# A plus-one by a ones matmul in PSUM, the first chunk pairs scaled straight from its bank, and TensorE's work put in another order

## The chip, the cores and the metric

The kernel runs on one core of one Trainium2 chip. The metric is the device time in microseconds (us). TensorE does the matmuls and the transposes, VectorE and ScalarE the elementwise work. Each execution also has a mean granted clock of TensorE, between 0.5 and 1.0 of full speed at any moment.

## The reference

One block of a diffusion transformer in bf16: 2 samples of 256 tokens, width 1152 (9 chunks of 128), hidden width 4608, 2 heads. Only the first lines matter here:

```python
mod = (_silu(c) @ w_mod).reshape(B, 6, 1, D)
shift_a, scale_a, gate_a, shift_m, scale_m, gate_m = [mod[:, i] for i in range(6)]
h = _layernorm(x, axis=-1) * (1 + scale_a) + shift_a
qkv = (h @ wqkv).reshape(B, N, 3, H, Dh)
# ... attention, output projection, second LayerNorm, two large matmuls
```

The tokens lie in four tiles of 128 (tiles 0 and 1 belong to sample 0, tiles 2 and 3 to sample 1). Each tile is normalised, transposed chunk by chunk by TensorE, and multiplied by `1 + scale_a` on its way from PSUM to SBUF ("modulated"); then the key projection starts on those chunks while more of `w_mod` is still arriving.

## The kernel before

`scale_a` is worked out in four groups of chunks, as each group's weights land. A group is a row of tiny matmuls (2 columns each) into a PSUM tile, and one instruction that adds one while it copies the result to SBUF. The small PSUM tiles share two banks in turn.

```python
def aux_tile(shape, name, dt=FP32):
    return psum.tile(shape, dt, name=name, tag="aux", bufs=2)

KGROUPS = [(0, 2), (2, 4), (4, 6), (6, 9)]

def scale_group(g):
    k0, k1 = KGROUPS[g]
    pm = aux_tile([P, k1 - k0, B], "pm")
    for j in range(k0, k1):
        for k in range(KD):
            nc.tensor.matmul(
                pm[:, j - k0, :], w_scale_a[:, k, j * P:(j + 1) * P], sT[:, k, 0:B],
                start=(k == 0), stop=(k == KD - 1),
            )

    def add_one(eng):
        dst = scale_a[:, k0:k1, :]
        if eng == "d":
            nc.vector.tensor_scalar_add(dst, pm[:], 1.0)
        else:
            nc.scalar.activation(dst, pm[:], ACT.Identity, bias=one_t[:])

    return add_one

def modulate(pt, i, k, t0, j0, w, eng):      # hT0 chunk k = transposed tile * (1 + scale)
    ...

def k_step(k, c0=0, c1=T, m0=0, m1=KM1):     # key matmuls of chunk k, tokens c0..c1
    ...
```

The stretch that the change reorders (`"a"` is ScalarE, `"d"` is VectorE; `P` is 128, `N` is 256; `warm` issues matmuls on zeros that only keep TensorE busy):

```python
    pt_0 = transpose_x([0, 1], [0])
    warm(4, pwarm)
    ...
    norm1(1, 0, CUT, "d")
    stats_aggregate(2)
    norm1(0, CUT, D, "d")
    scale_group(0)("a")
    for k in range(2):
        modulate(pt_0, k, k, 0, 0, P, "a")
    warm(1, pwarm)
    pt_1 = aux_tile([P, 1, 8 * P], "pt", BF16)
    for k in range(2):
        transpose_into(pt_1, k, k, 1)
    for k in (2, 3):
        for t in range(TPB):
            transpose_into(pt_1, 2 * (k - 1) + t, k, t)
    for k in range(2):
        modulate(pt_1, 0, k, 1, k * P, P, "d")
    sqrt1(2)
    k_step(0, 0, P)
    k_step(1, 0, P)
    ...
    norm1(2, 0, CUT, "d")
    k_step(0, P, N)
    k_step(1, P, N)
    ...
    for k in range(2):
        transpose_into(pt_1, 6 + k, k, 2)
    for k in range(2):
        modulate(pt_1, 0, k, 2, (6 + k) * P, P, "a")
    scale_group(1)("a")
    sqrt1(3)
    for k in (2, 3):
        modulate(pt_1, 0, k, 0, 2 * (k - 1) * P, N, "d")
    k_step(0, N, N + P)
    k_step(1, N, N + P)
    recip1(3)
    norm1(3, 0, CUT, "d")
    k_step(2, 0, N)
    ...
```

## Time and profile before

| | before |
|---|---|
| median of the 3 runs on hand first | 243.79 us (243.61 to 243.87) |
| span of the profiled run | 242.1 us |
| TensorE busy | 235.3 us, 97% |
| first scale weights landed, second, third group | 9.09, 12.17, 15.26 us |
| third scale group starts on TensorE | 15.57 us |

The page lists an engine's busy time; at 97% TensorE, a change counts by what it does to TensorE's work and to its remaining idle time. The chain of waits, in order of time, lists start, duration, engine, tile and line; each row is what released the next. The lines of both views stand in the prediction.

### The profile page before, as it was taken

How to read it: one execution, taken by the hardware profiler on the slowest of the kernel's cores; microseconds unless marked ns; L12 is line 12 of the kernel's file. 1: busy time of each engine (PE TensorE's matmuls, PEld its weight loads, DVE VectorE, ACT ScalarE, POOL GpSimd, SP SyncE). 2: the span in 40 equal slices, each digit the busy share in tenths (PEclk: the TensorE clock that was granted, in tenths of full speed). 3: DMA queues.
4: the chain of work that ended last, by engine and by line, in shares of the span. 5: the costliest groups of instructions: out<-in, count | busy, mean ns of one | idle time of the engine just before them, and what ended most of it. 6: DMA issues, size and time to landing. Idle time of an engine off the chain costs nothing.

```text
span 242.1 us, 4031 instructions
## 1 busy us (share of the span) xinstructions
PE 235.3 (97%) x1698; PEld 142.7 (59%) x1698; DVE 93.4 (39%) x209; ACT 69.5 (29%) x138; POOL 32.0 (13%) x48
## 2 busy tenths in 40 slices
PE   8799999999999999999999999999999999999994
PEld 2486444466656666888844444444566656665573
DVE  2872550675694676720000019999002000000001
ACT  6532250543735174782222233322000000000000
POOL 1000400000310616300000000000314111111111
PEclk9999999999999999999999999999999999999999
DMA  6999999999999999799999999996891000000000
GB/s 223 324 330 360 379 344 247 326 372 284 254 322 361 380 255 208 208 219 327 327 328 249 191 274 328 327 326 188 245 286 39 19 16 16 20 20 27 19 19 16
DMA packets 76989, 54.48 MB, mean 225 GB/s; under 512 B 26011, under 2 KB 72491, under 8 KB 76971
## 3 DMA queue, kind: packets, MB, share of 16 engines
q1 hardware_dynamic: 76240, 53.02, 77.7%
q0 software_dynamic: 704, 1.20, 1.6%
q8 instruction: 13, 0.21, 0.4%
q14 instruction: 5, 0.04, 0.0%
q10 hardware_dynamic: 27, 0.00, 0.0%
HBM read 46.90 MB, written 1.19 MB: 199 GB/s over the span
## 4 chain that ended last, share of the span: by engine, by line
PE 91%; DMA 3%; ACT 2%; DVE 2%; issue 0%; SPq 0%; DVEq 0%
PE pacc L866 29%; PE pacc L802 29%; PE pacc L584 7%; PE pacc L705 6%; PE pacc L511 5%; PE pk L288 4%; DMA w_scale_a<-in_w_mod_dram 3%; PE pacc L519 2%; PE pk L318 2%; ACT hT L687 2%; PE pa L619 1%; PE ps_s L539 1%; PE pn L432 1%; PE pm L248 1%; PE pt L266 1%; PE pg L467 1%
## 5 line engine op out<-in xcount | busy, mean ns | idle before, releaser
L802 PE MATMUL pacc<-hT,w_f 128*128 128x256 bf16 (+1 forms) x432 | 70.5, 326 | 0.2 <-ACT hT L687 0.2
L866 PE MATMUL pacc<-w_f,gT 128*128 128x384 bf16 (+2 forms) x468 | 70.5, 314 | 0.0
L866 PEld LDWEIGHTS <-gT 128*128 128x128 bf16 x468 | 44.4, 98 | 26.2
L802 PEld LDWEIGHTS <-w_f 128*128 128x128 bf16 x432 | 42.2, 98 | 28.0 <-issue 0.4
L485 DVE SCALAR_TENSOR_TENSOR late<-w_gate_mT,late 128x1152 bf16<-128x1152 bf16 x18 | 24.4, 1358 | 36.8 <-DMA w_gate_mT<-in_w_mod_dram 36.2
L872 DVE TENSOR_TENSOR tmp<-pacc,gate 128x384 f32<-128x384 f32 (+2 forms) x13 | 6.8, 527 | 62.5 <-PE pacc L866 50.5
L840 ACT ACTIVATE gT<-pacc 128x512 bf16<-128x512 f32 x24 | 14.3, 597 | 32.3 <-PE pacc L802 32.3
L485 DVE SCALAR_TENSOR_TENSOR s_spill<-w_scale_m,s_b 128x1152 bf16<-128x1152 bf16 x12 | 16.3, 1357 | 8.5 <-DMA w_scale_m<-in_w_mod_dram 8.2
L705 PE MATMUL pacc<-w_o,big 128*128 128x384 bf16 (+2 forms) x117 | 17.9, 314 | 0.0
L874 POOL TENSOR_TENSOR o_sb<-tmp,x 128x384 bf16<-128x384 f32 (+1 forms) x12 | 11.7, 974 | 47.4 <-DVE tmp L872 47.4
L584 PE MATMUL pacc<-w_v,hT 128*128 128x384 bf16 x108 | 17.9, 326 | 0.0
L705 PEld LDWEIGHTS <-big 128*128 128x128 bf16 x117 | 11.0, 98 | 6.8 <-ACT big L627 0.2
L584 PEld LDWEIGHTS <-hT 128*128 128x128 bf16 x108 | 10.4, 98 | 7.0 <-issue 0.2
L288 PE MATMUL pk<-big,w_k 128*128 128x128 bf16 (+2 forms) x102 | 13.3, 278 | 0.0
L711 POOL TENSOR_TENSOR x<-tmp,x_sb 128x384 f32<-128x384 f32 (+1 forms) x11 | 9.8, 891 | 17.4 <-DVE tmp L710 9.5
L511 PE MATMUL pacc<-hT,w_q 128*128 128x512 bf16 x54 | 11.8, 379 | 0.1
L327 POOL DMA_DIRECT2D gates_dram<-grow x4 | 2.1, 521 | 70.8 <-DVE grow L826 70.8
L818 ACT ACTIVATE gT<-pacc 128x512 bf16<-128x512 f32 x12 | 6.9, 597 | 10.4 <-PE pacc L802 10.4
L288 PEld LDWEIGHTS <-w_k 128*128 128x128 bf16 x102 | 7.8, 98 | 3.0
L511 PEld LDWEIGHTS <-w_q 128*128 128x128 bf16 x54 | 5.3, 98 | 6.7 <-issue 0.4
L710 DVE TENSOR_TENSOR tmp<-pacc,gate 128x384 f32<-128x384 f32 (+2 forms) x13 | 6.7, 522 | 5.4 <-PE pacc L705 5.2
L523 ACT ACTIVATE big<-pacc 128x512 bf16<-128x512 f32 x9 | 4.8, 608 | 11.5 <-PE pacc L511 8.8
(101 smaller groups left out, 160.9 us busy)
## 6 DMA issues: line engine op xcount, KB each, us to landing
w_f<-in_w_fc_dram SPq DMA_DIRECT2D x14, 864.0 KB, 11.0
w_f<-in_w_fc_dram SPq DMA_DIRECT2D x2, 2592.0 KB, 10.7
w_f<-in_w_fc_dram SPq DMA_DIRECT2D x2, 1728.0 KB, 13.8
w_shift_a<-in_w_mod_dram SPq DMA_DIRECT2D x3, 864.0 KB, 10.5
w_v<-in_wqkv_dram SPq DMA_DIRECT2D x3, 864.0 KB, 6.0
w_gate_a<-in_w_mod_dram SPq DMA_DIRECT2D x3, 864.0 KB, 9.2
w_o<-in_wo_dram SPq DMA_DIRECT2D x3, 864.0 KB, 6.2
w_shift_m<-in_w_mod_dram SPq DMA_DIRECT2D x3, 864.0 KB, 13.0
```

What stands on the lines that cost most here:

```text
L288: nc.tensor.matmul(pk[m][:, c0:c1], w_k[:, k, m * P:(m + 1) * P], hT0[:, k, c0:c1], start=(k == 0 and c0 == 0), stop=(k == KD - 1), skip_g ...
L485: nc.vector.scalar_tensor_tensor(spill, wT[:, j, :], 1.0, s_b[b], op0=ALU.mult, op1=ALU.mult, accum_out=dst(j, b),)
L511: nc.tensor.matmul(pq[m][:], w_q[:, k, m * P:(m + 1) * P], hT[:, k, :], start=(k == 0), stop=(k == KD - 1),)
L584: nc.tensor.matmul(pacc[:], hT[:, k, t * P:(t + 1) * P], w_v[:, k, pnl * PW:(pnl + 1) * PW], start=(k == 0), stop=(k == KD - 1),)
L705: nc.tensor.matmul(pacc[:], aT[:, k, t * P:(t + 1) * P], w_o[:, k, c0:c1], start=(k == ks[0]), stop=(k == ks[-1]),)
L711: (nc.vector if (t, i) in ((1, 2), (3, 3)) else nc.gpsimd).tensor_tensor(x1[:, t, c0:c1], tmp[:], x_sb[:, t, c0:c1], op=ALU.add)
L802: nc.tensor.matmul(dst, w_f1[m // KD][:, k, ml * P:(ml + 1) * P], hT[:, k, c0:c1], start=(k == 0), stop=(k == KD - 1),)
L818: nc.scalar.activation(gT[:, ms[0]:ms[-1] + 1, b * N:(b + 1) * N], pacc[:], ACT.Gelu_apprx_tanh)
L840: nc.scalar.activation(gT[:, m, :], pacc[:], ACT.Gelu_apprx_tanh)
L866: nc.tensor.matmul(pacc[:], gT[:, kk, t * P:(t + 1) * P], w_f2[j][:, r, c0 - n * PW:c0 - n * PW + cw], start=(kk == 0), stop=(kk == KF - 1),)
L872: nc.vector.tensor_tensor(tmp[:], pacc[:], gate_m[:, b, c0:c0 + cw], op=ALU.mult)
L874: (nc.vector if last else nc.gpsimd).tensor_tensor(o_sb[:], tmp[:], x1[:, t, c0:c0 + cw], op=ALU.add)
```

## The change

The intent: take ScalarE's plus-one out of the chain between the first scale matmuls and the first modulation. A ones matmul first fills the PSUM tile with ones, the scale matmuls accumulate on it, and VectorE modulates the first two chunk pairs with the scalar read straight from PSUM. ScalarE takes tile 1's first chunks, and several pieces of TensorE's work move to other places. The core of the diff:

```diff
-    one_t = const.tile([P, 1], FP32, name="one_t")
-    nc.vector.memset(one_t[:], 1.0)
+    ones_r = const.tile([1, P], BF16, name="ones_r")
+    nc.vector.memset(ones_r[:], 1.0)
 ...
+    def scale_group_matmuls(g):
         pm = aux_tile([P, k1 - k0, B], "pm")
+        nc.tensor.matmul(
+            pm[:].rearrange("p j b -> p (j b)"), ones_r[:, 0:P], ones_r[:, 0:(k1 - k0) * B], start=True, stop=False,
+            skip_group_check=True,
+        )
 ...
-                    start=(k == 0), stop=(k == KD - 1),
+                    start=False, stop=(k == KD - 1), skip_group_check=True,
 ...                                       # add_one becomes copy_out: plain copies
-    stats_aggregate(2)
-    norm1(0, CUT, D, "d")
-    scale_group(0)("a")
+    pm_0 = scale_group_matmuls(0)
     for k in range(2):
-        modulate(pt_0, k, k, 0, 0, P, "a")
-    warm(1, pwarm)
+        nc.vector.tensor_scalar_mul(hT0[:, k, 0:P], pt_0[:, k, 0:P], pm_0[:, k, 0:1])
+    nc.scalar.copy(scale_a[:, 0:2, :], pm_0[:])
 ...
     for k in range(2):
         transpose_into(pt_1, k, k, 1)
-    for k in (2, 3):
-        for t in range(TPB):
-            transpose_into(pt_1, 2 * (k - 1) + t, k, t)
-    for k in range(2):
-        modulate(pt_1, 0, k, 1, k * P, P, "d")
+    modulate(pt_1, 0, 0, 1, 0, P, "a")
+    stats_aggregate(2)
     sqrt1(2)
-    k_step(0, 0, P)
-    k_step(1, 0, P)
+    modulate(pt_1, 0, 1, 1, P, P, "a")
 ...
-    k_step(0, P, N)
-    k_step(1, P, N)
+    k_step(0, 0, P)
+    k_step(1, 0, P)
 ...
     for k in range(2):
         transpose_into(pt_1, 6 + k, k, 2)
+    k_step(0, P, N)
+    for k in (2, 3):
+        for t in range(TPB):
+            transpose_into(pt_1, 2 * (k - 1) + t, k, t)
+    k_step(1, P, N)
     for k in range(2):
         modulate(pt_1, 0, k, 2, (6 + k) * P, P, "a")
-    scale_group(1)("a")
+    k_step(0, N, N + P)
+    pm_1 = scale_group_matmuls(1)
+    for k in (2, 3):
+        nc.vector.tensor_scalar_mul(
+            hT0[:, k, 0:N], pt_1[:, 0, 2 * (k - 1) * P:2 * k * P], pm_1[:, k - 2, 0:1]
+        )
+    nc.scalar.copy(scale_a[:, 2:4, :], pm_1[:])
     sqrt1(3)
-    for k in (2, 3):
-        modulate(pt_1, 0, k, 0, 2 * (k - 1) * P, N, "d")
-    k_step(0, N, N + P)
-    k_step(1, N, N + P)
     recip1(3)
     norm1(3, 0, CUT, "d")
+    k_step(1, N, N + P)
 ...                                       # norm1(0, CUT, D) moves to behind tile 3's modulation
```

## The prediction

> **What bounds the kernel now.** I read the page first, then the chain that ended last in order of time for the first 34 us, then the merged timeline of 8 to 17 us, then each load's landing, and last the built order of both kernels with what each instruction waits for.
>
> The page says who sets the end:
>
> ```profile
> PE 235.3 (97%) x1698; PEld 142.7 (59%) x1698; DVE 93.4 (39%) x209; ACT 69.5 (29%) x138; POOL 32.0 (13%) x48
> ...
> PE 91%; DMA 3%; ACT 2%; DVE 2%; issue 0%; SPq 0%; DVEq 0%
> ```
>
> TensorE is the bound nearly everywhere, so the time moves by what the change adds to or takes from TensorE's idle time, unless a later idle absorbs it. All of the edit lies between 8 and 20 us. The chain there, in order of time (start, us, what):
>
> ```profile
> 1.66 7.42 DMA w_scale_a<-in_w_mod_dram
> 9.09 0.05 issue
> 9.13 0.62 PE pm L248 x18
> 9.75 0.02 issue
> 9.77 0.27 ACT scale_a L258
> 10.05 0.02 issue
> 10.07 0.64 ACT big L275 x2
> 10.71 0.47 DVE big L273 x2
> 11.17 0.47 DVE stats L188
> 11.64 0.07 DVE rstd L222
> 11.71 0.03 issue
> 11.74 0.42 DVE xn L235
> 12.16 0.05 issue
> 12.21 0.28 PE pt L358 x2
> 12.49 0.43 PE pm L248 x18
> 12.92 0.03 issue
> 12.95 1.94 PE pk L288 x21
> ...
> 15.57 0.59 PE pm L248 x18
> ```
>
> The reader is to see three things. The start hangs on the first scale weights (they land at 9.09). From 9.75 to 12.21 the chain runs through ScalarE and VectorE: plus-one, modulation of tile 0, modulation of tile 1, normalisation of tile 2. From 12.21 on it is almost all TensorE up to the end, with pauses of only 0.1 to 0.3 us each in the next 20 us. So the change has about 3 us in which to win or lose, and what it loses there stays lost: in the rest of the chain only one TensorE wait is listed (0.2 us, at 98.7 us, on ScalarE), and it hangs on TensorE's own earlier work, so it moves along.
>
> TensorE's idle time from 9.60 (last scale matmul issued) to 15.57 (start of the third scale group), from issue times against the regular pitch (56 ns per 128-column matmul, 109 per 256, 25 per scale matmul): 0.49 before 10.09 (filled by one warming matmul), 0.07 at 10.49, 0.38 at 12.21, 0.17 at 12.95, 0.13 at 13.75, 0.18 at 15.57. Sum 1.42 us. Loads are near: the landings of the scale groups are 9.09, 12.17, 15.26 and 19.11, used at 9.13, 12.33, 15.57 and 20.17. Even a perfect edit could bring the third group only from 15.57 to about 15.3.
>
> **What the Trainium skill says.** "PSUM — Partial Sum Buffer", section "PSUM bank collisions raise a hardware error", has two engines kept off one bank by semaphores per bank, reads against reads included. The build does this. The trace agrees: tile 1's modulation on VectorE reads columns written by the first two of six transposes, yet starts at 10.69, after the last of them (10.09+0.49=10.58). The same page, "The four PSUM rules", says that any non-zero seed must be put there by TensorE with the clearing flag; the ones matmul does that, so the result should be right; no run here shows it yet. "TensorEngine Tiling (Array Packing)", section "Tiling Modes", says that a change of tiling mode drains TensorE. The trace agrees: on entering the 64-row matmuls of the scores at 54.78 the issue comes 0.10 us late against the pitch and on leaving at 55.33 0.15 us late; 32-column groups give 0.09 and 0.12 us. The ones matmul has one row and is built as a 32-row tile, so it pays this on both sides.
>
> **The change part by part**, on the clock of before, with durations of its trace. Waits are from the built order; a semaphore hop costs 0.04 to 0.06 us there (pm ends 9.736, ScalarE starts 9.774; norm ends 12.148, TensorE starts 12.205), 0.11 where an engine needs a separate wait instruction first.
>
> 1. First pair. The ones matmul of group 0 lies in the wait for the load: free. ScalarE's plus-one (0.27) leaves the path: VectorE starts at 9.78 from PSUM, a 128x128 pair takes 0.48 there as now, ends 10.25. But the second transposed tile now gets the bank that tile 0's transposes held, not the scale's, and so waits for those two VectorE reads: transposes of tile 1 start at 10.31 instead of 10.09. Only two of the six stand there, so the first key matmuls start at 10.48, as before (10.49). Gain 0.
>
> 2. Tile 1 by ScalarE. It first copies the scale (it must wait for VectorE to leave that bank: 10.35 to 10.62), then modulates chunk 0 (0.37, to 11.03), takes the square root of tile 2 (to 11.2), then chunk 1 (to 11.45). VectorE meanwhile is free for tile 2: reciprocal 11.24 to 11.38, normalisation 0.41, end 11.83, against 12.15 before: 0.32 earlier. But TensorE has only 12 key matmuls (0.67) to do after 10.48 and is out of work at 11.15. It waits for tile 2's normalisation until 11.89: idle 0.74. Before, 24 stood there.
>
> 3. Next: two transposes, six matmuls, four transposes, six matmuls: 0.12+0.34+0.22+0.34, to 12.91. ScalarE's tile 2 modulation must now wait for all of these transposes (one bank): 12.77, first done 13.14, so TensorE goes on at 13.19: idle 0.28.
>
> 4. Group 1 is moved behind six of these matmuls: ones at 13.52, the 18 matmuls to 14.03 (done 14.17), six more to 14.37. VectorE scales chunks 2 and 3 from PSUM: 14.28, first done 14.63 (0.35), second 14.89; before they ran at 13.34. TensorE starts chunk 2 at 14.68 (before 13.75): idle 0.32.
>
> 5. ScalarE's copy waits for both of these reads (14.99 to 15.25), and tile 3's square root stands behind the copy: 15.44. Then reciprocal 15.63, normalisation to 16.08; before 14.47. TensorE has nine 256-column matmuls (0.98), is out of work at 15.66 and waits until 16.14: idle 0.48. Then transposes (0.11), three matmuls (0.33), four transposes (0.22), to 16.80, and group 2 waits for tile 3's modulation by VectorE (16.94): 16.99, idle 0.19.
>
> Idle by this count: 0.71 before 10.31, 0.07, 0.74, 0.28, 0.32, 0.48, 0.19 = 2.79 against 1.42: 1.37 us lost.
>
> 6. Ones matmuls of groups 1, 2 and 3 stand on TensorE's path. Each costs entry 0.1, its own slot of some 0.03 and leaving 0.12: an estimate of 0.25; group 2's entry falls in idle, so 0.65 for the three if the full toll is paid, 0.1 if it isn't. I take 0.45.
>
> 7. The moved normalisation of tile 0's second part (0.38) falls behind tile 3's modulation on VectorE: four of them end at 18.3, needed by transposes at about 18.8. Hidden, by 0.5. The plain copies cost as much as the adds.
>
> After group 2 the rest is the same work on TensorE, later by the whole amount; the loads only gain slack, and the store of the condition row and the loads behind it move along. Sum: 1.37+0.45 = 1.8 us: 243.8+1.8 = 245.6.
>
> **Rivals.**
> (a) As intended: ScalarE's step gone, first pair sooner, 0.3 to 0.5 us gained: 243.4. For it: 0.27+0.05 us of plus-one truly stand in the chain, and tile 2's normalisation does come 0.32 sooner. Against it: TensorE can't use this, for its filler (tile 1's 12 matmuls and 4 transposes) now lies behind that same normalisation; and the third group's load at 15.26 caps any gain at 0.3.
> (b) Hidden anyway: the delays of steps 4 and 5 are smaller than worked out and the loads set the rhythm, 243.5 to 244.3. For it: the loads are 0.2 to 0.3 us from binding. Against it: from 15.5 to 33 us before is TensorE without a pause, so only what comes before counts, and tile 3's square root has moved behind the copy in the built order, which is no matter of estimate.
> (c) Worse: a scalar pointer into PSUM slows VectorE's modulations, or each change of tile mode waits for a full drain (a 128-column matmul lasts 0.22 against a pitch of 0.06): 0.2 to 0.7 more, 246.3. The trace of before has no VectorE instruction with such a pointer, so this is open.
>
> **Range and chances.** Steps 1 to 5 rest on built waits and measured durations: I allow 0.4 either way, and 0.35 for the ones matmuls; runs of before differ by 0.26. So 245.6, range 244.7 to 246.3. Two per cent is 4.9 us, over twice the loss that I find and well over ten times any gain that the loads permit: faster 0.01, within 0.97, slower 0.02.
>
> **What would show it.** Right: first key matmuls at about 10.5; a TensorE idle of about 0.7 before tile 2's transposes at 11.9; chunk 2's matmuls near 14.7 to 14.9; tile 3's transposes near 16.1 to 16.4, behind ScalarE's square root, itself behind the copy; group 2 near 17 to 17.4; the same TensorE stretch after that, all later by one amount. Wrong: if tile 3's square root comes before 14.5, or if group 2 starts by 16, the loss isn't there; if the 25 ns pitch goes on across the ones matmul, step 6 is too large; if the pair on VectorE at 9.78 takes 0.6 or more, rival (c) holds; if the shift at 34 us is not found again at the end, something later absorbs it.

## The result, and the profile after

| | median | lowest to highest | runs |
|---|---|---|---|
| before | 243.88 us | 243.61 to 244.28 | 6 |
| after | 245.50 us | 244.98 to 246.98 | 6 |

The ratio of the times is 1.0076 with a 95% interval of 1.0047 to 1.0106: slower by 0.8%, within the 2% that counts as the same. A ratio is the mean time of one kernel's fast runs over that of the other's fast runs of the same rounds, so it isn't quite the ratio of the medians.

The page of the changed kernel, with each engine's busy time and the shares of the chain that ended last:

```profile
PE 236.6 (97%) x1692; PEld 144.0 (59%) x1701; DVE 93.7 (38%) x209; ACT 69.3 (28%) x138; POOL 31.9 (13%) x48
...
PE 93%; DMA 3%; DVE 2%; issue 1%; ACT 0%; SPq 0%; DVEq 0%; ACTq 0%
```

The fall of ScalarE's share (2% to 0%) doesn't come from the plus-one. Most of the 2% was ScalarE's modulation of the second LayerNorm near 95 us in the kernel before:

```profile
94.48 3.06 ACT hT L687 x6
...
97.72 0.99 ACT hT L687 x2
```

In the changed kernel's profile TensorE comes there later, and the chain goes through it instead. In the stretch that was changed, ScalarE has as much of the chain as ever: 0.27 and 0.64 us before (the prediction shows the rows), 0.37, 0.19, 0.16 and 0.20 us now. What did go is the plus-one between the first scale matmuls and the first modulation: VectorE starts at 9.68 us, 0.02 us after the end of the scale matmuls (9.04 + 0.62). TensorE's busy time rose by 1.3 us. Four ones matmuls, less one warming matmul, can't be that much. The chain of the changed kernel in order of time (start, us, what) shows where the time went. L363 and L395 are VectorE's modulations with the scalar from PSUM, L368 the transposes, L287 ScalarE's modulation, L235 a normalisation, L300 key matmuls, L398 ScalarE's copy of the scale, L219 a square root, L246 a ones matmul:

```profile
9.68 0.49 DVE big L363 x2
...
10.22 0.28 PE pt L368 x2
...
10.59 0.37 ACT big L287
10.96 0.19 ACT rstd L219
...
11.37 0.42 DVE xn L235
...
11.84 0.40 PE pt L368 x2
...
13.30 1.28 PE pk L300 x12
...
15.37 0.63 DVE big L395 x2
...
16.08 0.16 ACT scale_a L398
16.24 0.20 ACT rstd L219
...
17.14 0.28 PE pt L278 x2
...
17.99 0.16 PE pm L246
```

The order of events is the predicted one, but from 11.84 on TensorE's rows are too long: twelve key matmuls of 128 columns in 1.28 us are 107 ns each, against the 56 ns of before. The busy time by stretches explains it. Columns: stretch, its length, then busy time (and instructions) of TensorE, its weight loads, VectorE, ScalarE and GpSimd, the granted clock, the share of the DMA engines and GB/s. The changed kernel:

```profile
8.22:11.63 3.41, 2.11 (x36) 1.40 (x33) 2.52 (x11) 1.26 (x5) 0.00 (x0) 1.00 1.11 327
11.63:15.05 3.42, 3.21 (x41) 3.00 (x41) 1.32 (x4) 0.62 (x2) 0.00 (x0) 0.50 1.12 323
```

And the kernel before, in a stretch just as long in nearly the same place:

```profile
7.83:11.24 3.41, 2.89 (x44) 1.88 (x42) 2.37 (x12) 1.65 (x7) 0.00 (x0) 1.00 1.12 332
```

The clock was halved from 11.63 to 15.05 us, for 3.41 us, after a stretch in which TensorE was busy for 2.11 us of 3.41, where before it was 2.89. The prediction has nothing of this. So two questions go to the chip: is it the order of work or the clock that costs the time, and does the clock fall in every run?

The mean clock of each run answers part of the second. A halving of 3.41 us takes some 0.007 off the mean: the profiled run has 0.991 and took 246.37 us; the other five have 0.997 to 1.000 and took 244.98, 245.28, 245.36, 245.63 and 246.98. So the profile shows the rarer case. The means of 0.997 to 0.999 are, in the profiles, only a clock that falls after the last matmul. Below, "full clock" are runs with a mean clock of 0.997 or more. None of the 40 runs of the kernel before that stand beside the experiments below is under that.

### The profile page after: what moved, and what is told of

Same layout as the page of the kernel before. It is cut to its first block, busy times and chain, and to the rows that moved or that the text cites.

```text
span 244.6 us, 4031 instructions
## 1 busy us (share of the span) xinstructions
PE 236.6 (97%) x1692; PEld 144.0 (59%) x1701; DVE 93.7 (38%) x209; ACT 69.3 (28%) x138; POOL 31.9 (13%) x48
## 4 chain that ended last, share of the span: by engine, by line
PE 93%; DMA 3%; DVE 2%; issue 1%; ACT 0%; SPq 0%; DVEq 0%; ACTq 0%
PE pacc L881 29%; PE pacc L817 29%; PE pacc L720 7%; PE pacc L599 7%; PE pacc L526 5%; PE pk L300 4%; DMA w_scale_a<-in_w_mod_dram 3%; PE pacc L534 2%; PE pk L330 2%; PE pa L634 1%; PE ps_s L554 1%; PE pn L447 1%; PE pm L252 1%; PE pt L278 1%; PE pg L482 0%
## 5 line engine op out<-in xcount | busy, mean ns | idle before, releaser
L300 PE MATMUL pk<-big,w_k 128*128 128x128 bf16 (+2 forms) x100 | 14.6, 293 | 0.3 <-DVE big L395 0.2
L300 PEld LDWEIGHTS <-w_k 128*128 128x128 bf16 x102 | 8.6, 107 | 3.1 <-issue 0.3
```

The lines of the kernel that those rows point to most:

```text
L300: nc.tensor.matmul(pk[m][:, c0:c1], w_k[:, k, m * P:(m + 1) * P], hT0[:, k, c0:c1], start=(k == 0 and c0 == 0), stop=(k == KD - 1), skip_g ...
```

## The experiments

My theory: the order of TensorE's work is the main cause (transposes and key matmuls that filled waits now stand behind them), with the ones matmuls second. The rivals: the clock is what costs the time, and with warming the change would be level or better; or a scalar read from PSUM, or ScalarE's part of tile 1, is what slows it.

| run | median | ratio, 95% | full-clock runs, median | runs below full clock |
|---|---|---|---|---|
| e0 changed kernel again | 245.25 | 1.0061, 1.0041 to 1.0081 | 245.12 (4) | 245.56, 246.13 |
| e1 with more warming | 245.28 | 1.0066, 1.0043 to 1.0089 | 245.28 (6) | none |
| e2 ones matmul alone on before | 243.95 | 1.0012, 0.9986 to 1.0037 | 243.95 (6) | none |
| e3 changed, without ones matmul | 245.18 | 1.0053, 1.0028 to 1.0078 | 244.73 (2) | 245.56, 245.70 |
| e4 square root early | 245.37 | 1.0064, 1.0040 to 1.0088 | 244.85 (2) | 245.75, 245.76 |
| e5 group 1 early | 245.12 | 1.0059, 1.0039 to 1.0079 | 244.86 (2) | 245.32, 245.69 |
| e6 fillers back | 245.26 | 1.0074, 1.0033 to 1.0115 | 244.97 (3) | 247.01 |
| e7 tile 1 on VectorE | 245.99 | 1.0097, 1.0079 to 1.0115 | 245.82 (1) | 245.85, 246.13, 246.34 |
| e8 = e4, e5 and e6 together | 243.85 | 1.0002, 0.9980 to 1.0023 | 243.85 (6) | none |
| e9 = e8, ones matmul for two groups only, warming | 243.86 | 1.0003, 0.9979 to 1.0027 | 243.86 (6) | none |
| e10 less warming | 246.05 | 1.0093, 1.0069 to 1.0116 | none | all 4 |
| e11 order alone on before | 244.49 | 1.0027, 1.0005 to 1.0049 | 244.49 (6) | none |

The kernel before had medians of 243.79 beside e0 to e3, 243.83 beside e4 to e7, 243.77 beside e8 to e10 and 243.63 beside e11. Where a run below full clock is among few, the median mixes two cases, so I compare full-clock runs, and give their number. Full-clock runs of one kernel scatter too (those of the kernel before lie between 243.32 and 245.06), so differences of 0.2 to 0.3 us between two to four runs carry little weight without a trace that shows the same.

In the profiles one distance measures the stage that matters: from the first scale matmul to the start of the third group, 6.44 us before.

### e0: the changed kernel again

No edit; it is there to be compared with the others on their own chip.

> The changed kernel unedited, as the control on this chip. My theory (TensorE runs out of work because fillers and group 1 were moved behind other engines' results, plus the toll of the ones matmuls): 245.0 to 245.7 in runs whose clock stays at 1.0, group 2 of the scale matmuls starting near 17.0 to 17.3 us. Clock-gate theory (the loss is mainly that the longer idles let the granted clock fall to a half, as the profile showed from 11.6 to 15.0 us): runs with mean clock under 0.995 are 0.7 to 1.2 us longer than those at 1.0, and it happens in some runs, not all; if the gate were the whole cause, runs at clock 1.0 would be at 243.9 to 244.3.

Measured: 245.25 us; the four full-clock runs 245.06 to 245.33, the two others 245.56 and 246.13, the profiled one among them. With the first six runs, three of twelve runs of the changed kernel had the clock halved. Here that cost 0.4 and 1.0 us against the full-clock median (0.7 to 1.2 were expected). The loss of 1.3 us that the full-clock runs show is something else.

### e1: keep the clock up

```diff
-    warm(4, pwarm)
+    warm(6, pwarm)
 ...
     pm_0 = scale_group_matmuls(0)
+    warm(2, pwarm)
```

> The changed kernel with four more warming matmuls (0.9 us) in places where TensorE idles anyway: two before group 0, while it waits for the load, two after it, while it waits for VectorE. My theory: at full clock the same time as the changed kernel, 244.9 to 245.5 (nothing on the path is longer), and the half clock between 8 and 20 us is gone from the profile and from every run, so that the spread falls from 2 us to under 0.7 us. Clock-gate-is-all theory: 243.9 to 244.3.

Measured: all six runs at full clock (busy 2.81 us in the stretch of 3.41 that starts at 8.08), and still 245.28 us. The clock is therefore not the main cause. The spread, 1.5 us where under 0.7 was expected, missed; the slowest run is looked at below. This run's chain is also the one on which the prediction's steps can be read undisturbed (its lines from 364 on are one higher):

```profile
11.90 0.28 PE pt L369 x2
...
12.78 0.38 ACT big L287
...
13.20 0.49 PE pk L300 x6
...
14.44 0.63 DVE big L396 x2
...
15.15 0.16 ACT scale_a L399
15.31 0.20 ACT rstd L219
...
16.21 0.28 PE pt L278 x2
...
17.06 0.16 PE pm L246
```

Each hop away from TensorE in these rows is a TensorE wait: on the normalisation before 11.90, on ScalarE's modulation of tile 2 before 13.20, on VectorE's pair at 14.44, and on the path copy, square root, normalisation before 16.21. The third group stands 8.06 us after the first scale matmul here; in after's profile, at half clock for a while, 9.04.

The medians hide one more thing. The profiled run of e1 is its slowest, 246.63 us. It lost 1.3 us near 99 us by its issue times (0.35 in the kernel before), where the transposed second LayerNorm is waited for and its transfer landed late, at 97.18. The waits between 95 and 105 us (line, what was waited for, us, times, longest):

```profile
PE pacc L818 <- ACT hT L703: 0.8, 3, 0.4
```

The view counts less of it than the issue times do; before, it counted 0.2 us. So this place can make runs vary too, apart from the change.

### e2: the ones matmul alone, on the kernel before

```diff
+        nc.tensor.matmul(
+            pm[:].rearrange("p j b -> p (j b)"), ones_r[:, 0:P], ones_r[:, 0:(k1 - k0) * B], start=True, stop=False,
+            skip_group_check=True,
+        )
 ...
-                    start=(k == 0), stop=(k == KD - 1),
+                    start=False, stop=(k == KD - 1), skip_group_check=True,
 ...
-                nc.vector.tensor_scalar_add(dst, pm[:], 1.0)
+                nc.vector.tensor_copy(dst, pm[:])
 ...
-                nc.scalar.activation(dst, pm[:], ACT.Identity, bias=one_t[:])
+                nc.scalar.copy(dst, pm[:])
```

> The kernel before, in its own order, with only the ones matmul in each scale group and plain copies in place of the adds. The ones matmul of group 0 lies in the wait for the load; those of groups 1, 2 and 3 are on the path at 0.2 each by the changed kernel's profile (0.10 on entering, 0.10 to the next issue). My theory: 0.4 to 0.6 us slower than before, 244.3 to 244.5, group 2 at about 15.7 and group 3 0.2 later still. Rival, the ones matmul is free: 243.9, group 2 at 15.5 to 15.6.

Measured: 243.95, +0.16 us, with an interval that holds 0. The median is a third of what was expected, but the interval reaches up to 0.9 us and doesn't exclude 0.4. The trace says more: TensorE's work after group 3 comes 0.23 us later than before. Up to the third group nothing is lost (it is at 6.45 us, as before): group 1's toll vanishes in a wait that stands there in the old order anyway. Of the 0.23 us, 0.19 is given back at the wait near 99 us.

### e3: the changed order without the ones matmul

```diff
-        nc.tensor.matmul(
-            pm[:].rearrange("p j b -> p (j b)"), ones_r[:, 0:P], ones_r[:, 0:(k1 - k0) * B], start=True, stop=False,
-            skip_group_check=True,
-        )
 ...
-                    start=False, stop=(k == KD - 1), skip_group_check=True,
+                    start=(k == 0), stop=(k == KD - 1),
```

This one leaves out the one of `1 + scale` and so gives a wrong result (relative error 0.70).

> The changed kernel without its ones matmuls, so with a wrong result on purpose (the scale lacks its one). My theory: 0.4 to 0.6 us faster than the changed kernel at the same clock, so 244.6 to 244.9, still 0.8 to 1.1 over before; group 2 near 16.8. Rival, that the ones matmuls are the main cost: 244.0 or under.

Measured: two full-clock runs, 244.66 and 244.80, so 0.4 less than e0. The traces of the changed kernel say the same from below: entering a ones matmul costs 0.095 us against the pitch and leaving it about 0.105, some 0.20 in all. Group 0 pays nothing (it waits for the load), group 2 only 0.09 (its entry lies in a wait), groups 1 and 3 pay in full: 0.5, of which 0.4 is seen here, though two runs against four can't settle it. The remaining +0.9 of e3 against before isn't the ones matmuls'; e8 and e11 show that it is the order.

### e4, e5, e6: undo one move each

e4 takes tile 3's square root out from behind ScalarE's copy:

```diff
         modulate(pt_1, 0, k, 2, (6 + k) * P, P, "a")
+    sqrt1(3)
     k_step(0, N, N + P)
 ...
     nc.scalar.copy(scale_a[:, 2:4, :], pm_1[:])
-    sqrt1(3)
```

> The changed kernel with tile 3's square root put ahead of the copy of group 1's scale on ScalarE, so that it needn't wait for VectorE's scaling of chunks 2 and 3. My theory: tile 3's normalisation ends some 0.5 to 0.7 us sooner, TensorE's idle of 0.38 before tile 3's transposes goes to under 0.1, group 2 starts 0.3 to 0.5 earlier than in the changed kernel at the same clock, time 0.3 to 0.5 less: 244.8 to 245.1. Rival (the square root's place doesn't matter, the transposes wait for TensorE itself): no change, 245.3.

Measured: full-clock runs 244.71 and 244.99, about 0.3 below e0. In its trace TensorE no longer waits before tile 3's transposes, and the third group stands at 8.41 us. The trace of e0, whose clock fell at the same distance from the first scale matmul (3.18 us in both), has 0.31 us of wait there, and 8.73. The median of 245.37 doesn't show it, as two of four runs were below full clock.

e5 puts group 1's matmuls back ahead of tile 2's key matmuls:

```diff
-    k_step(0, N, N + P)
     pm_1 = scale_group_matmuls(1)
+    k_step(0, N, N + P)
```

> The changed kernel with the scale matmuls of group 1 back ahead of the six key matmuls of tile 2's chunk 0. They then fill TensorE's wait for ScalarE. My theory: the idle of 0.33 before chunk 2's matmuls and that of 0.28 before chunk 0 of tile 2 shrink to under 0.2 together, chunks 2 and 3 are scaled 0.5 to 0.7 sooner, group 2 starts 0.4 to 0.7 earlier, time 244.6 to 245.0. Rival, that the load of group 1 would bind in its new place (it lands at 12.1): no gain, 245.3.

Measured: full-clock runs 244.80 and 244.92, again about 0.3 below e0, again with two of four below full clock. Its profile is of a halved clock and can't be compared with e1's.

e6 puts the fillers back: the four transposes of chunks 2 and 3 and tile 1's key matmuls ahead of tile 2's transposes.

```diff
     for k in range(2):
         transpose_into(pt_1, k, k, 1)
+    for k in (2, 3):
+        for t in range(TPB):
+            transpose_into(pt_1, 2 * (k - 1) + t, k, t)
 ...
-    for k in range(2):
-        transpose_into(pt_1, 6 + k, k, 2)
     k_step(0, P, N)
-    for k in (2, 3):
-        for t in range(TPB):
-            transpose_into(pt_1, 2 * (k - 1) + t, k, t)
     k_step(1, P, N)
+    for k in range(2):
+        transpose_into(pt_1, 6 + k, k, 2)
```

> The changed kernel with the four transposes of chunks 2 and 3 and the twelve key matmuls of tile 1 back ahead of tile 2's transposes. My theory: TensorE's idle before tile 2's transposes (0.84 in the profile) falls under 0.3 and it stays busy enough to keep the clock; tile 1's scaling by ScalarE must wait for all six transposes (one bank), 0.2 to 0.3 later. Group 2 starts 0.4 to 0.7 earlier than in the changed kernel at full clock, time 244.6 to 245.0, and no run shows a clock under 0.995. Rival: ScalarE's later scaling of tile 1 eats it up, 245.2 to 245.4.

Measured: full-clock runs 244.68, 244.97 and 245.56, about 0.2 below e0, less than I had expected, and one run at a mean clock of 0.983, which I had expected not to occur. The idle before tile 2's transposes is gone and the third group stands at 7.72 us (8.06 in e1), but ScalarE's modulation of tile 2 now makes TensorE wait 0.62 us, as nothing is left to do there.

Taken alone the three moves give back some 0.3, 0.3 and 0.2: for the first and the last the traces show a third group that is 0.3 us sooner, for e5 there are only its two runs.

### e7: tile 1's first chunks on VectorE

```diff
-    modulate(pt_1, 0, 0, 1, 0, P, "a")
+    modulate(pt_1, 0, 0, 1, 0, P, "d")
 ...
-    modulate(pt_1, 0, 1, 1, P, P, "a")
+    modulate(pt_1, 0, 1, 1, P, P, "d")
```

> The changed kernel with tile 1's first chunks scaled by VectorE again, as before. My theory: this part of the change helps: without it VectorE gets to tile 2's normalisation about 0.4 us later, so tile 2's transposes start 0.3 to 0.5 later (12.1 to 12.3) and the time is 0.2 to 0.5 longer, 245.5 to 245.9 at full clock. Rival, that ScalarE was the wrong engine for it: 244.9 or less.

Measured: 245.99; its one full-clock run, 245.82, is 0.7 above e0. Tile 2's transposes stand at 12.18 us instead of 11.90. The third group is at 8.46 us instead of 8.06, at full clock in both traces. So ScalarE's part is a gain of some 0.4 us by the trace: VectorE normalises tile 2 earlier, and the rival that blames ScalarE falls.

### e8: all three moves undone, ones matmul and PSUM scalars kept

The edit is those of e4, e5 and e6 together.

> The changed kernel with all three moves of order undone together: the fillers (four transposes, twelve key matmuls) ahead of tile 2's transposes, group 1 ahead of tile 2's key matmuls, tile 3's square root ahead of the copy. The ones matmuls, the scaling straight from PSUM, and tile 1 on ScalarE stay. My theory (the order is the main cause, the ones matmuls a small one): nearly all of the loss goes, group 2 starts 6.2 to 6.6 us after the first scale matmul (before 6.4, the changed kernel at full clock 8.0), time 243.8 to 244.3, 0.0 to 0.2 per cent over before. Rival (the bank waits of the new PSUM reads are the main cause): still over 244.6.

Measured: 243.85 us against 243.77, ratio 1.0002, with no run below full clock. Its chain:

```profile
10.11 0.49 PE pt L368 x6
10.60 1.45 PE pk L300 x24
12.05 0.18 PE pt L368 x2
12.24 0.11 PE pm L246
12.34 0.54 PE pm L252 x18
12.88 1.68 PE pk L300 x21
...
15.23 0.16 PE pm L246
```

From 10.11 to 14.5 us the chain is TensorE without a pause: 24 key matmuls stand where the changed kernel has 12, and tile 2's normalisation is ready before they end. The third group is at 6.40 us, level with before. Everything that is new in the changed kernel except the three moves is in this one, and the loss is gone. Together the moves give back 1.3 us where alone they gave 0.8 in sum: the waits are in series, and undoing one lets TensorE run into the next, as e6's 0.62 us shows.

### e9: the best mix that I found

It is e8 with the warming of e1, and with the ones matmul only for the groups whose scalar is read from PSUM:

```diff
+        if g < 2:
             nc.tensor.matmul(
                 ...
-                    start=False, stop=(k == KD - 1), skip_group_check=True,
+                    start=(g >= 2 and k == 0), stop=(k == KD - 1), skip_group_check=True,
 ...
-                nc.vector.tensor_copy(dst, pm[:])
+                nc.vector.tensor_scalar_add(dst, pm[:], 1.0)
```

> As the last, with the ones matmul only in groups 0 and 1, where TensorE waits anyhow, VectorE adding the one in groups 2 and 3 as before, and four warming matmuls in idle places. This is meant to be the best of both. My theory: the load of the third scale group (it lands 6.1 us after the first) permits 0.2 to 0.3 at most, so 243.5 to 243.9, not distinguishable from before; if it is 243.2 or less, the parts of the change that I call worthless (scaling from PSUM, tile 1 on ScalarE) are worth something once the order is right.

Measured: 243.86 us, ratio 1.0003, interval 0.9979 to 1.0027. The third group came to 6.30 us, 0.13 sooner than before; in the time this can't be told from nothing. It can hardly become much more, since the third group's weights land 6.2 us after the first in all other profiles. But the distance flatters e9. Its first weights landed at 8.37, and the warming kept TensorE from the first scale matmul until 8.81; counted from that landing, the third group is at 6.75 us, in the kernel before at 6.48. So the warming may have cost something too, and e9 doesn't show what the mix is worth without it. No version that was run beats the kernel before.

### e10: less warming

```diff
     pt_0 = transpose_x([0, 1], [0])
-    warm(4, pwarm)
```

> The changed kernel without the four warming matmuls ahead of group 0, so that TensorE is idle for 1.3 us longer there. Clock-gate theory: the half clock comes in most or all runs (it came in 3 of 12 of the changed kernel and in none of 6 with warming added), mean clock under 0.995, time 245.6 to 246.4. If it doesn't come more often, the fall of the clock has nothing to do with TensorE's idle time.

Measured: 246.05 us, all four runs below full clock. The busy time by stretches of its profiled run:

```profile
8.43:11.84 3.41, 1.57 (x33) 1.33 (x34) 2.23 (x10) 0.97 (x4) 0.00 (x0) 1.00 1.12 326
11.84:15.26 3.42, 3.42 (x45) 3.21 (x46) 1.09 (x3) 0.63 (x2) 0.00 (x0) 0.50 1.11 323
```

Again one stretch of 3.41 us at half clock, behind one with little TensorE work. Without the four warming matmuls on zeros the clock always fell (4 of 4), with them sometimes (3 of 12), with eight never (0 of 6); at 3 of 12, six runs without a fall would come by chance about once in six tries, so the last step is likely but not shown.

### e11: the order alone, on the kernel before

```diff
-    warm(4, pwarm)
+    warm(6, pwarm)
 ...
-    for k in (2, 3):
-        for t in range(TPB):
-            transpose_into(pt_1, 2 * (k - 1) + t, k, t)
 ...
-    k_step(0, P, N)
-    k_step(1, P, N)
 ...
         transpose_into(pt_1, 6 + k, k, 2)
+    k_step(0, P, N)
+    for k in (2, 3):
+        for t in range(TPB):
+            transpose_into(pt_1, 2 * (k - 1) + t, k, t)
+    k_step(1, P, N)
 ...
+    k_step(0, N, N + P)
     scale_group(1)("a")
 ...
-    k_step(0, N, N + P)
     k_step(1, N, N + P)
```

This has two of the three moves; tile 3's square root stays early. It has no ones matmul and no PSUM scalar: plus-one and modulations are as before.

> The kernel before with two of the changed kernel's moves of order and nothing else of it: the fillers behind tile 2's transposes and group 1 behind tile 2's first key matmuls (plus two warming matmuls in the wait for the first load, so that the clock holds). No ones matmul, no scaling from PSUM, no tile 1 on ScalarE, and tile 3's square root doesn't wait for VectorE. My theory (order suffices): TensorE stands idle for some 0.8 before tile 2's transposes, group 2 starts 7.1 to 7.6 after the first scale matmul (before 6.4), time 244.4 to 244.9. Rival (the order costs only because of the new PSUM reads and ScalarE's part): 243.7 to 244.0.

Measured: 244.49 us against 243.63, all six runs at full clock. The ratio of the means is smaller than that, 1.0027 (0.7 us), as the kernel before had runs of up to 245.06 on this chip; its whole interval is above 1. Its chain:

```profile
11.07 0.41 DVE xn L235
...
12.84 0.49 PE pk L288 x6
...
14.51 1.14 PE pk L288 x9
...
16.33 0.59 PE pm L248 x18
```

The same waits come up: TensorE at 12.84 behind ScalarE's modulation, at 14.51 behind VectorE's. The third group is 7.64 us after the first scale matmul. The order makes the kernel slower without any other part of the change (two moves give 0.7 us, between 0.1 and 1.2), and e8 shows the rest doing no harm, to within 0.6 us, without the order.

## Why the prediction was right

The prediction said 245.6 us, slower by less than 2%; 245.50 was measured, and the range of 244.7 to 246.3 holds it. The mechanism was the right one, but the closeness is partly luck: two things that it didn't have pull in opposite directions. I go through its steps on e1, which is the changed kernel at full clock.

**Steps 1 to 5, the idle time.** Predicted and measured starts: tile 1's transposes 10.31 and 10.27; tile 2's transposes 11.89 and 11.90; ScalarE's tile 2 at 12.77 and 12.78; TensorE on at 13.19 and 13.20; chunk 2's matmuls 14.68 and 14.85; tile 3's transposes 16.14 and 16.21; third group 16.99 and 17.06. The waits after the first transposes came out at 0.85 (predicted 0.74), 0.28 (0.28), 0.33 (0.32), 0.38 (0.48) and 0.18 (0.19), in sum 2.02 against 2.01. The first of all, 0.71 before 10.31, is partly filled by the warming in e1; e8, without it, has 0.72. These steps held, and e8 and e11 show them to be the cause. The wait per PSUM bank, on which steps 1 and 3 rest, was read from a doubtful case: the profile puts VectorE's start at 10.69 down to ScalarE, which ended in the same moment. e8 settles it. There ScalarE reads what the first two of six transposes wrote, and starts at 10.70, 0.10 us after the last of the six (10.11 + 0.49).

**Step 6, the ones matmuls.** Taken as 0.45, measured as 0.5 from the issue times and, in few runs, 0.4 from e3 against e0. The result was right in every experiment but e3, which leaves them out, as the prediction expected.

**The sum.** In e1 TensorE begins the matmuls of the attention's shift, well behind the fourth group, at 33.13 us; before it was 31.32. That is 1.81 later, where the prediction had 1.8.

**Step 7.** "The plain copies cost as much as the adds" was wrong: ScalarE's copy of 128x4 took 0.16 us, its add with a bias 0.26. It has no weight, since the copy comes after a wait.

**"What it loses there stays lost" was wrong by some 0.2 us.** The wait near 99 us hangs on a transfer as well as on TensorE, and takes up part of a delay: in e0's profile the changed kernel was 2.49 us late ahead of it, and 2.30 late at the second large matmul. At full clock the end is later by 1.3 (e0), 1.5 (e1) and 1.5 us (245.36 against 243.88 in the first six), not by 1.8; what the wait doesn't explain of this is no more than the scatter of runs.

**The clock is missing altogether.** It fell in 3 of 12 runs of the changed kernel, and those took 0.4 to 1.0 us more than full-clock runs. They lift the median of the first six runs by only 0.14 (245.36 without the low run, 245.50 with it), but they fill the upper part of the range. The Trainium skill's page "TensorE: Matmul & The Clock Gate", section "Part 1: The HAM clock gate (the "warmup" mystery)", would have told me to look: a monitor judges TensorE's activity over free-running windows of 3413 ns and grants half or full speed. The traces agree on both numbers, 3.41 us at 0.5, and in each profile the clock's changes lie whole multiples of 3.41 us apart (in the changed kernel's, 228.69 us, 67 of them, from the rise at 15.05 to the fall behind the last matmul). As the windows run free of the kernel, the same kernel meets them in different places, which fits a clock that falls in some runs only; no run here moves the window on purpose, so this stays an inference.

**The rivals.** (a), a gain as intended, is refuted by every run of the changed kernel; even e9 shows no gain. (b), hidden anyway, is refuted by e1 and e11. (c), a slow scalar from PSUM, is refuted by the durations of single instructions. VectorE's modulations by form, in the changed kernel (busy us, mean ns of one, idle before):

```profile
L363 DVE TENSOR_SCALAR big<-pt,pm 128x128 bf16<-128x128 bf16 x2 | 0.5, 284 | 0.4 <-PE pm L252 0.4
```

and in the kernel before, with the scalar in SBUF:

```profile
L273 DVE TENSOR_SCALAR big<-pt,scale_a 128x128 bf16<-128x128 bf16 x4 | 1.0, 281 | 1.5 <-ACT big L275 0.9 <-PE pt L266 0.6
```

284 ns against 281. The other half of (c), that each change of tile mode waits for a full drain and costs 0.2 to 0.7 us more, falls with the toll of 0.5 us in step 6.

**What stays open.** Full-clock runs have outliers for which there is no trace (246.98 of the changed kernel, 245.10 of e2, 245.06 of the kernel before); the late transfer of e1's profiled run is a candidate, not shown for the others. What exactly the clock gate counts isn't settled either: the profiles give bounds only, and e6's low run, which had the fillers in place and a mean clock of 0.983, has no trace.

## What to carry to other kernels

When you take an instruction off the path that leads to the bound engine, list what that engine still has to do in each wait of the new order: here 0.3 us of ScalarE went away, and the fillers that covered the other waits went behind them. Count waits per PSUM bank, since a tile that moves to the other bank inherits the other bank's readers (here tile 1's transposes: 10.27 us in e1, 10.09 before). And leave some spare work in early waits: here a stretch that was short of matmuls could cost twice, once as idle time and once more as a halved clock.

## What the Trainium skill lacked or had wrong

- "TensorE: Matmul & The Clock Gate", section "Why this matters for your kernels", asks for no gaps beyond about 3 us between bursts of matmuls. That is too lax: here the clock was halved after windows in which TensorE was busy for 1.57 (e10), 1.71 (e5), 1.93 (e0), 1.99 (e4), 2.11 (the changed kernel) and 2.16 us (e3) of 3.41, with no gap over 0.9 us in the changed kernel's profile and none over 1.5 us in that of e10. It stayed up after windows with 2.19 (e10, the one from 5.02 us), 2.21 (e7) and 2.38 us (e11), and in all profiles after every fuller one. The page says elsewhere that short idles between groups of matmuls can make the clock swing, but gives no share. A rule by busy share is wanted; these numbers bound it between 2.16 and 2.19 of 3.41 us for this kernel alone, with the windows placed by the clock's own changes.
- "TensorEngine Tiling (Array Packing)", section "Tiling Modes", says that a change of mode drains TensorE, without a figure. Here entering a one-row matmul cost 0.095 us and leaving it about 0.105, so 0.20 for a single seed matmul in the midst of 128-row ones.
- "VectorE: DVE Perf Modes", section "Scalar operands", doesn't say what a per-partition scalar costs when it lies in PSUM. Here it was nothing visible: 284 against 281 ns for 128x128, 350 against 346 ns for 128x256, with the tile itself in PSUM in both.
